# A new order of issue with a table of buffers, one pool of eight PSUM banks, and global scores issued tile by tile

## The chip, the cores and the metric

The kernel runs on one core of a Trainium2 chip, as one launch. The metric is the device time of an execution in microseconds (us). PE is TensorE, which runs the matmuls, PEld its weight loads, DVE VectorE, ACT ScalarE, POOL GpSimd, and SP the queue that issues nearly all DMAs. Each engine works through its own list of instructions in the order in which the kernel emits them, and waits on semaphores where it needs another engine's result or a buffer that another engine has yet to leave.

## What is computed

Three stages follow each other, with 4 batches of 544 tokens (512 local and 32 global) and 512 features:

```python
# 1. attention, 8 heads of 64: global queries see all keys, local ones a band of 65 and the 32 global keys
out_g = sm(scale * q_g @ k_all.T) @ v_all
s_ll = where(|i - j| <= 32, scale * q_l @ k_l.T, -1e9)
out_l = sm(concat(scale * q_l @ k_g.T, s_ll)) @ concat(v_g, v_l)
x = concat(out_g, out_l)
# 2. four experts, each a causal attention of width 64, weighted by a top-2 gate
for e in range(4):
    out += gate_e(x) * (softmax(causal(x @ wq[e], x @ wk[e])) @ (x @ wv[e])) @ wo[e]
# 3. a feed-forward with a token shift
xk = mu_k * x + (1 - mu_k) * x_prev
xr = mu_r * x + (1 - mu_r) * x_prev
return sigmoid(xr @ w_r) * (relu(xk @ w_k) ** 2 @ w_v)
```

(In the kernel local tokens stand ahead of global ones in a row of scores where that makes the band contiguous. Products that need more than one rounding's precision are made of three matmuls of a high and a low part.)

## The kernel before

All engine calls go to a recording layer. `Log` keeps each call as (engine, name, arguments) in a list, and tiles are `Lazy`: a tile is allocated when the first call that uses it is emitted. At the end `nc.emit(sequence(ORDER))` emits the calls in the order of the numbers in `ORDER`, a long table of steps between positions in the list. So `ORDER`, and nothing else, sets what stands behind what on each engine and in the DMA queue. The recording is done by ordinary loops:

- **Attention** (`a_` and `g_` functions). A pair P of heads has its queries and keys in one tile `kq{P}` (688 KB) and its values in `vw{P}`. `a_qk(n)` makes the local scores of a half pair: 8 matmuls into two tiles `S{n}_0` and `S{n}_1`, one for each head; DVE then masks and takes the minimum (`mn{n}`), ACT takes the exponential, DVE the reciprocal, POOL normalises (`pn{n}`, `glob`), PE transposes (`pT{n}`, and `pTg{u}` for `glob`), ACT or DVE copies the transposes out, and `a_pv(u)` multiplies by the values into `x{u}0`, `x{u}1` and `xg{u}`. `g_qk(u)` makes the global scores of two pairs (four heads): for each head a matmul of 32 x 512 into `Sga{u}` and one of 32 x 32 into `Sgb{u}`. Heads sit at partitions 0 or 64 of `kq`, and a head's 32 global queries fill 32 of the 128 rows of `Sga{u}`. So the four heads use four different places of PE's array: 64 rows by 32 columns each.
- **Experts** (`b_`, `c_`, `l_`, `e_`). `b_v` and `b_qk` make values (`pv`) and queries and keys (`pb..q`, `pb..k`). `c_qk(b, ep, i)` makes causal scores `C{b}{ep}{i}0` and `..1` of 128, 256, 384 or 512 columns; mask and minimum on DVE (`csm`, `cmn`), exponential on ACT, normalising on POOL, transposes `cT` on PE, copies `cpt` on ACT and DVE, and `c_pv` into `y`. `e_wo` (tiles `po`) is the output projection. Beside this stage the weights of stage 3 are loaded and split into a high and a low part (`wraw`, `wg`, `wy`) by ACT, DVE and POOL.
- **Feed-forward** (`d_`). Tokens in four blocks of 512 and one of 128: `d_mix` (tiles `m0`, `m1`), `d_k`, `d_v`, `d_r`, `d_out`.

PSUM has eight banks, and every tile in it fills one. `ps_s` and `ps_t` hand out six of them (tag `a`) in rotation: scores, transposes, projections. `ps_x` hands out two (tag `x`) to the accumulators of `a_pv`, `c_pv` and half of `d_v`. SBUF tags rotate in the same way: the n-th tile of a tag with k buffers takes the one that was handed out k tiles earlier. A matmul that starts a new tile waits until the last reader of the bank's former tile, a DVE or ACT instruction, is done.

Of the kernel before, what the change touches and what calls it, by code (L numbers as in the profile page):

```python
# [9 lines left out]
F32 = mybir.dt.float32  # L10
# [7 lines left out]
B, H, SL, SG, HD = 4, 8, 512, 32, 64  # L18
# [58 lines left out]
class LazyPool:  # L77

    def __init__(self, pool):
        self.pool = pool  # L80

    def tile(self, shape, dt, **kwargs):
        return Lazy(lambda: self.pool.tile(shape, dt, **kwargs), np.broadcast_to(np.float32(0), shape))
# [29 lines left out]
def chain_kernel(ctx: ExitStack, tc: tile.TileContext, kq, vw, vgd, wqkv, pack, wo, w_k, w_v, w_r, c_causal, out):  # L113
    nc = Log(tc.nc)
# [16 lines left out]
    def ps_s(name):  # L131
        return ps.tile([128, 512], F32, tag="a", bufs=6, name=name)

    def ps_t(name):
        return ps.tile([128, 512], F32, tag="a", bufs=6, name=name)

    def ps_x(name):
        return ps.tile([128, 512], F32, tag="x", bufs=2, name=name)
# [854 lines left out]
0 17 1 584 -592 -13 16 -17 13 -2 -2 -4 8 -21 8 2 -3 10 -19 1x2 1 -2 190 -195 18x2 1 44 -50 49 -46x2 96 -97x4 -8 7x3 1  # L993
21 99 -100x2 -26 25 -20 -3 2x2 153 -154 -8 -2 8x4 2 -14 14 67 -67 -16 8 11x4 -11 37x2 -7 -22 27x2 -8 7x2 -48 47x3 -10
-21x2 -8 -10 16x2 14 -15x4 22 2 -15 31 -44 -28 49 -23 -14 48 -9 -28 35x2 -51 40 9 -14 3 -26 -3 23 3 1 -32 29 1 30 -62
61x3 -34 4 53x4 -29 -26x4 -42 41x5 -28 34 9 -15 14 -19 18 -19 18 1 -15 -4 -2 4 13 1x2 -25 24x4 -21 20x3 -28 38 -11
10x3 141 -221 40 27 18x2 25 -49 22 -25 24 24 -38 54x2 -66 46 18x6 -78 15 2 34 -20 -19 18 -50 49x5 13 -14x2 -26 1 73
-48 109 -63 -73 72 -52 51 -49 49 -78 25 51x3 -12 11x4 -61 60x3 -89 88 -19 -32 -58 57x3 19 -54 61 17x2 -48 47 -86 85x8
-90 89 -41 40x2 -69 -24 44 19 -42 172 -173 377 -378 125 -103 102 -101 -53 152 -108 107 -102 -9 45x4 -69 68x2 -42 -23
63x6 -93 92 -69 68x3 -75 74x4 -95 94x3 -80 79x3 -70 69 79 -77 19 -88 -4 90 -19 -7x2 66 -42 28x2 11 -12x2 -53 29 -30 16  # L1000
-17x4 -11 10x3 24x2 30 -56 24x2 -28 4 22x2 -108 107x2 -29 2 5 -3 178 -177 24 -25 17 -18 -14 31 19 2 -19 -4 21x2 -44 43
-57 39x2 9 -10x2 84x4 -75 74 -88 87 -54 53x3 -93 92x3 -111 60x2 -61 60 -12 11 -48 -29 63 -36 46 -31x6 14 -15x2 2 -42
51 -3 -65 66x3 -14 2 20x2 14 -44 28x2 -24 23x2 11 -12x3 11 -47 35 30x2 44 -45x2 -27 26 -34 -4 36x3 -35 34x4 -63 20
41x2 -36 4x2 134 -135 -14 13 -7 -45 77x3 -30 29 -37 36x4 -40 39x3 -88 87x6 -76 75x2 31 -32x3 -80 79x3 -82 81 8x2 15
-145 128x2 68 -69x2 -80 79x2 2 -101 120 -36 -125 141 18x2 -24 49 -27x2 -29 -135 162x2 23 -24x2 -26 5 21 -22 -148 133
# [111 lines left out]
-25x11 -93 92 -93x11 16 -17 16x3 -19 18x3 -21 20x3 -23 22x2 4 -5 4x3 -7 6x3 -9 8x3 -11 10x26 50 -51 50x2 -26 25 -26x4  # L1117
22 -23x7 6 -7 6x2 -8 7 -8x2 12 -13 12 -8 7x2 -15 14
"""


def _constants():
    neg = np.float32(NEG)
# [67 lines left out]
```

## Time and profile before

| what | us |
|---|---|
| median of three runs | 554.11 |
| the three runs | 553.34 to 554.89 |
| the profiled execution | 553.6 |
| its span, first to last instruction | 551.8 |
| PE busy in the span | 524.6 (95%) |
| DVE, ACT, POOL busy | 319.5, 318.6, 303.7 (58%, 58%, 55%) |
| DMA: 51 MB, mean rate | 92 GB/s |

A busy share is the time in which at least one instruction of the engine is under way. A PE matmul is pipelined: the next may start before the last has ended, and the idle time that the profile names counts from the modelled end of the last. The chain of work that ended last lies on PE for 78% of the span. Attention ends at about 120 us, the experts at about 312 us, and the feed-forward takes the rest; the first two overlap for some 30 us, since `ORDER` mixes them.

### The profile page before, as it was taken

How to read it: one execution, taken by the hardware profiler on the slowest of the kernel's cores; microseconds unless marked ns; L12 is line 12 of the kernel's file. 1: busy time of each engine (PE TensorE's matmuls, PEld its weight loads, DVE VectorE, ACT ScalarE, POOL GpSimd, SP SyncE). 2: the span in 40 equal slices, each digit the busy share in tenths (PEclk: the TensorE clock that was granted, in tenths of full speed). 3: DMA queues.
4: the chain of work that ended last, by engine and by line, in shares of the span. 5: the costliest groups of instructions: out<-in, count | busy, mean ns of one | idle time of the engine just before them, and what ended most of it. 6: DMA issues, size and time to landing. Idle time of an engine off the chain costs nothing.

```text
span 551.8 us, 11621 instructions
## 1 busy us (share of the span) xinstructions
PE 524.6 (95%) x4286; PEld 429.8 (78%) x4286; DVE 319.5 (58%) x1065; ACT 318.6 (58%) x891; POOL 303.7 (55%) x361
## 2 busy tenths in 40 slices
PE   5899989999999999999798999999999999999996
PEld 2666677888878888888686788888888888888885
DVE  3667557587798879789878742415430367253011
ACT  4888567577677697687577664604541257233020
POOL 3768653738558888889677834505450376142110
PEclk9999999999999999799889999999999999999999
DMA  8958335005303454242722002001000100020002
GB/s 331 398 196 273 122 104 166 17 3 171 127 29 97 136 208 136 103 128 77 279 93 88 1 0 78 0 20 58 1 1 1 57 20 0 2 76 20 0 1 77
DMA packets 16025, 50.99 MB, mean 92 GB/s; under 512 B 1760, under 2 KB 2400, under 8 KB 15328
## 3 DMA queue, kind: packets, MB, share of 16 engines
q1 hardware_dynamic: 15680, 49.98, 25.9%
q8 instruction: 34, 0.56, 0.4%
q10 hardware_dynamic: 288, 0.26, 0.1%
q14 instruction: 23, 0.19, 0.1%
HBM read 39.49 MB, written 10.75 MB: 91 GB/s over the span
## 4 chain that ended last, share of the span: by engine, by line
PE 78%; DVE 9%; ACT 7%; POOL 3%; issue 1%; DMA 1%; ACTq 0%; DVEq 0%; POOLq 0%
PE v L100 17%; PE k L100 16%; PE r L100 8%; PE x L100 4%; PE S L100 4%; PE po L100 3%; PE pv L100 3%; PE y L100 3%; PE cT L100 3%; PE Sga L100 3%; PE C L100 3%; PE pT L100 2%; POOL csm L100 2%; ACT csm L100 2%; PE xg L100 1%; ACT sm L100 1%
## 5 line engine op out<-in xcount | busy, mean ns | idle before, releaser
L100 POOL TENSOR_TENSOR kk<-k,kk 128x512 fp32r<-128x512 f32 x32 | 41.7, 1311 | 92.9 <-ACT kk L100 92.8
L100 DVE TENSOR_TENSOR k<-k 128x512 f32<-128x512 f32 x34 | 29.3, 864 | 85.1 <-ACT k L100 84.6
L100 ACT ACTIVATE sm<-sm,mn 128x160 f32<-128x160 f32 x128 | 53.5, 420 | 24.4 <-DVE mn L100 21.0
L100 DVE SCALAR_TENSOR_TENSOR mm<-xT,small,mt 128x32 f32<-128x32 f32 (+7 forms) x64 | 48.5, 798 | 24.1 <-POOL m1cpt L100 12.5
L100 POOL TENSOR_TENSOR csm<-csm,crc 128x256 f32<-128x256 f32 (+3 forms) x64 | 51.9, 828 | 17.5 <-DVE crc L100 11.6
L100 POOL TENSOR_TENSOR pn<-sm,rc 128x256 f32<-128x256 f32 x64 | 38.6, 617 | 16.3 <-PE pT L100 6.5
L100 ACT ACTIVATE k<-k 128x512 f32<-128x512 f32 x34 | 20.3, 596 | 44.1 <-PE k L100 37.5
L100 DVE CUSTOM_DVE_ANT_0 sm<-S,band 128x160 f32<-128x160 f32 x128 | 35.2, 318 | 18.1 <-PE S L100 17.7
L100 PE MATMUL v<-wv1H,kk 128*128 128x512 f32 x136 | 43.6, 389 | 0.0
L100 PE MATMUL v<-wv0H,kk 128*128 128x512 f32 x136 | 43.5, 389 | 0.0
L100 ACT ACTIVATE csm<-csm,cmn 128x128 f32<-128x128 f32 (+3 forms) x64 | 35.8, 564 | 13.3 <-DVE cmn L100 12.9
L100 ACT ACTIVATE mt<-xT,omu 128x32 f32<-128x32 f32 (+7 forms) x64 | 31.6, 519 | 14.6 <-DVE mm L100 14.4
L100 POOL TENSOR_TENSOR m1cpt<-mm,m1vC 128x512 fp32r<-128x512 f32 x16 | 21.7, 1374 | 30.9 <-ACT m1vC L100 23.1
L100 DVE CUSTOM_DVE_ANT_0 csm<-C,causal 128x128 f32<-128x128 f32 (+3 forms) x64 | 29.9, 483 | 8.8 <-PE cT L100 4.8
L100 ACT CAST kk<-k 128x512 fp32r<-128x512 f32 x32 | 19.4, 620 | 24.2 <-PE v L100 13.6
L100 PE MATMUL S<-kq 64*64 64x160 f32 x512 | 27.1, 317 | 6.4 <-DMA kq<-in_kq_dram 4.9
L100 POOL TENSOR_TENSOR m0L<-mm,m0H 128x512 fp32r<-128x512 f32 (+1 forms) x20 | 25.2, 1271 | 14.2 <-ACT m0H L100 14.1
L100 DVE TENSOR_TENSOR rt<-v,rt 128x512 f32<-128x512 f32 x17 | 11.6, 686 | 36.0 <-PE v L100 26.3
L100 PE MATMUL y<-cpt,vC 128*64 128x128 f32 (+1 forms) x320 | 30.0, 313 | 2.2 <-DVE cpt L100 1.0
L100 PE MATMUL cT<-ident,csm 128*128 128x128 f32 x160 | 27.4, 288 | 4.2 <-POOL csm L100 2.0
L100 POOL TENSOR_TENSOR glob<-sm,rc 128x128 f32<-128x128 f32 x32 | 12.8, 403 | 33.9 <-DVE rc L100 23.1
L100 PEld LDWEIGHTS v<-wv0H,kk 128*128 128x128 f32 x136 | 25.5, 188 | 5.3
(316 smaller groups left out, 1582.8 us busy)
## 6 DMA issues: line engine op xcount, KB each, us to landing
kq<-in_kq_dram SPq DMA_DIRECT2D x15, 688.0 KB, 5.5
vw<-in_vw_dram SPq DMA_DIRECT2D x16, 512.0 KB, 4.5
out_dram<-rt SPq DMA_DIRECT2D x17, 256.0 KB, 2.0
wrawv<-in_moe_w_v_dram SPq DMA_DIRECT2D x8, 512.0 KB, 3.8
wrawk<-in_moe_w_k_dram SPq DMA_DIRECT2D x8, 512.0 KB, 4.1
wrawr<-in_moe_w_r_dram SPq DMA_DIRECT2D x4, 512.0 KB, 3.8
dv0H<-wgv SPq DMA_DIRECT2D x4, 256.0 KB, 2.8
dv0L<-wyv SPq DMA_DIRECT2D x4, 256.0 KB, 3.0
```

The lines of the kernel that those rows point to most:

```text
L100: getattr(getattr(self.nc, engine), name)(*[now(x) for x in args], **{k: now(x) for k, x in kwargs.items()})
```

## The change

Four things:

1. `LazyPool.tile` no longer lets a tag rotate. A table `SLOTS` names for each tag, tile by tile in the order of emission, which buffer it takes.
2. `ps_s`, `ps_t` and `ps_x` share one tag, `bank`, of eight banks; the table gives each of its 463 tiles one.
3. `g_qk` emits the four `Sga` matmuls of its four heads and then the four `Sgb`, where before each head's `Sgb` followed its `Sga`.
4. `ORDER` is a new table.

```diff
     def tile(self, shape, dt, **kwargs):
+        if kwargs.get("bufs", 1) > 1:
+            tag = kwargs["tag"]
+            n = self.count[tag] = self.count.get(tag, -1) + 1
+            kwargs.update(tag=tag + SLOTS[tag][n], bufs=1)
         return Lazy(lambda: self.pool.tile(shape, dt, **kwargs), np.broadcast_to(np.float32(0), shape))
...
     def ps_s(name):
-        return ps.tile([128, 512], F32, tag="a", bufs=6, name=name)
+        return ps.tile([128, 512], F32, tag="bank", bufs=8, name=name)
...
     def ps_x(name):
-        return ps.tile([128, 512], F32, tag="x", bufs=2, name=name)
+        return ps.tile([128, 512], F32, tag="bank", bufs=8, name=name)
...
-        for pp in range(2):
-            t = kqs[2 * u + pp]
-            for h in range(2):
-                rr = slice(64 * h, 64 * h + 64)
-                oo = slice(32 * (2 * pp + h), 32 * (2 * pp + h) + 32)
-                k = t[rr, KT0:KT0 + 768].rearrange("p (g c) -> p g c", c=96)[:, :, 0:64]
-                nc.tensor.matmul(sa[oo, :], t[rr, QG0:QG0 + SG], k, start=True, stop=True)
-                nc.tensor.matmul(sb_[oo, 0:SG], t[rr, QG0:QG0 + SG], t[rr, KT0 + 64:KT0 + 96], start=True, stop=True)
+        hs = [(kqs[2 * u + n // 2], slice(64 * (n % 2), 64 * (n % 2) + 64), slice(32 * n, 32 * n + 32)) for n in range(4)]
+        for t, rr, oo in hs:
+            k = t[rr, KT0:KT0 + 768].rearrange("p (g c) -> p g c", c=96)[:, :, 0:64]
+            nc.tensor.matmul(sa[oo, :], t[rr, QG0:QG0 + SG], k, start=True, stop=True)
+        for t, rr, oo in hs:
+            nc.tensor.matmul(sb_[oo, 0:SG], t[rr, QG0:QG0 + SG], t[rr, KT0 + 64:KT0 + 96], start=True, stop=True)
...
 ORDER = """
-0 17 1 584 -592 -13 16 -17 13 -2 -2 -4 8 -21 8 2 -3 10 -19 1x2 1 -2 190 -195 18x2 1 44 -50 49 -46x2 96 -97x4 -8 7x3 1
...
+SLOTS = {
...
+    "kp": "03210321032103210321",
...
```

What the new order does is read from the built programs. In the rows below a number behind a tile's letter is its index in the kernel (`Sga3` is `g_qk(3)`), and the number behind the last underscore is the tile's own. The line is that of the recording layer, and it stands four lines lower in the changed kernel. `x2` is two equal instructions in a row.

PE in the first third of attention, around the global scores of pairs 6 and 7, before:

```order
L100 MATMUL pT9_820<-ident_105,pn9_710 128x128 x4
L100 MATMUL Sga3_834<-kq6_345 32x512
L100 MATMUL Sgb3_836<-kq6_345 32x32
L100 MATMUL Sga3_834<-kq6_345 32x512
L100 MATMUL Sgb3_836<-kq6_345 32x32
L100 MATMUL Sga3_834<-kq7_405 32x512
L100 MATMUL Sgb3_836<-kq7_405 32x32
L100 MATMUL Sga3_834<-kq7_405 32x512
L100 MATMUL Sgb3_836<-kq7_405 32x32
L100 MATMUL x10_620<-tg1_655,vgb_152 128x512
```

and now:

```order
L104 MATMUL xg1_589<-ptlg_103,vw2_182 64x32
L104 MATMUL Sga3_712<-kq6_311 32x512 x2
L104 MATMUL Sga3_712<-kq7_364 32x512 x2
L104 MATMUL Sgb3_720<-kq6_311 32x32 x2
L104 MATMUL Sgb3_720<-kq7_364 32x32 x2
L104 MATMUL S12_0_726<-kq6_311 64x160
```

The four 32x512 matmuls now stand in one row. Before, `g_qk(3)` and `g_qk(6)` alone had their two pairs side by side; the two pairs of each of the other six stood apart, 8 to 130 matmuls of other work between them, and once a pair of one call stood beside a pair of another. Now all eight calls have the form shown.

PE later in attention, at local scores that take over a bank, before (`S19_0` takes the bank of `S18_1`, and `pv00` that of `S19_0`):

```order
L100 MATMUL pT15_1201<-ident_105,pn15_1098 128x128 x4
L100 MATMUL S18_0_1210<-kq9_706 64x160
L100 MATMUL S18_1_1212<-kq9_706 64x160
...
L100 MATMUL S19_0_1225<-kq9_706 64x160
L100 MATMUL S19_1_1227<-kq9_706 64x160
...
L100 MATMUL pv00_1241<-wv_929,x00_1094 128x260 x12
```

and now (`pv00` takes the bank of `Sga5`, and `S19_0`, further down, that of `pb01k0`):

```order
L104 MATMUL S18_1_1147<-kq9_664 64x160
L104 MATMUL Sga5_1162<-kq10_963 32x512 x2
L104 MATMUL Sga5_1162<-kq11_944 32x512 x2
L104 MATMUL Sgb5_1174<-kq10_963 32x32 x2
L104 MATMUL Sgb5_1174<-kq11_944 32x32 x2
L104 MATMUL pb01q0_1179<-x00_1113,wq_412 128x256 x12
L104 MATMUL pv00_1205<-wv_1036,x00_1113 128x260 x12
L104 MATMUL pb01k0_1231<-x00_1113,wk_818 128x256 x12
L104 MATMUL pv01_1257<-wv_1036,x00_1113 128x260 x12
L104 MATMUL pT14_1281<-ident_111,pn14_1109 128x128 x4
```

The projections have moved in between. Before, no matmul stood between the last one into `S18_1` and the first into `S19_0`, and one between `S19_0` and `pv00`; now 16 stand between `Sga5` and `pv00`, and 24 between `pb01k0` and `S19_0`.

PE in the experts' stage, where the scores of batch 3 begin, before (`C3011` takes the bank of `cT2120`):

```order
L100 MATMUL cT2120_4427<-ident_105,csm2120_4273 128x128 x3
L100 MATMUL cT2111_4434<-ident_105,csm2111_4214 128x128 x2
L100 MATMUL pb31k1_4438<-x31_4183,wk_763 128x288 x12
L100 MATMUL cT2121_4471<-ident_105,csm2121_4237 128x128 x3
L100 MATMUL C3010_4485<-qk30_3873 128x256
L100 MATMUL C3011_4487<-qk30_3873 128x256
```

and now (`C3011` takes the bank of `y203`):

```order
L104 MATMUL y203_4444<-cpt203_4175,vC2_3312 64x160 x8
L104 MATMUL y203_4444<-ptl2_4298,vl_2551 64x32 x2
L104 MATMUL C3000_4467<-qk30_3905 128x128
L104 MATMUL C3001_4469<-qk30_3905 128x128
...
L104 MATMUL cT2121_4483<-ident_111,csm2121_4245 128x128 x3
L104 MATMUL cT2120_4490<-ident_111,csm2120_4260 128x128 x3
L104 MATMUL C3010_4503<-qk30_3905 128x256
L104 MATMUL C3011_4505<-qk30_3905 128x256
```

The bank that `C3011` takes over was emptied before by ACT, and now by ACT and DVE, with 13 matmuls between where there were 18.

Counted over both whole programs: a bank passes from one tile to the next 455 times. Fewer than 6 matmuls stood in between 11 times before and never now, fewer than 12 matmuls 53 times before and 16 times now. Between the local scores of a half pair and their transposes stood 99 matmuls (median of 32), now 141; the fewest were 24 and are 48. Between causal scores and their transposes stood 92 (median of 64), now 111; the fewest were 46 and are 56. On DVE, as its list is printed with equal rows in one, 135 rows lay between the first mask of `C200` and that of `C300`, and 126 do now.

## Rows read from the trace of the kernel before

**Rows 1.** Table by stretch: us, busy (instructions) per engine, granted PE clock, DMA share, GB/s

```profile
0.00:120.00 120.00, 108.46 (x1580) 79.06 (x1581) 74.52 (x424) 82.79 (x314) 69.67 (x131) 1.00 0.52 185
120.00:200.00 80.00, 77.69 (x795) 68.02 (x795) 64.70 (x240) 58.46 (x166) 57.99 (x66) 1.00 0.36 117
200.00:312.00 112.00, 103.06 (x819) 87.62 (x818) 96.22 (x290) 84.80 (x227) 89.03 (x94) 0.94 0.35 123
312.00:547.00 235.00, 234.87 (x1097) 195.01 (x1096) 82.72 (x115) 92.54 (x186) 87.01 (x71) 1.00 0.06 21
```

**Rows 2.** PE's waits, whole run: waiting group <- releaser, us in total, times, longest

```profile
PE S L100 <- DMA kq<-in_kq_dram: 4.9, 1, 4.9
PE pT L100 <- POOL pn L100: 2.4, 2, 1.5
PE C L100 <- ACT cpt L100: 1.9, 1, 1.9
PE C L100 <- DVE qk L100: 1.4, 1, 1.4
...
PE pv L100 <- DVE mn L100: 0.9, 1, 0.9
```

**Rows 3.** Groups by line and form, global scores: busy us, mean ns, idle before

```profile
L100 PE MATMUL Sga<-kq 64*32 64x512 f32 x64 | 17.4, 630 | 0.0
L100 PE MATMUL Sgb<-kq 64*32 64x32 f32 x64 | 4.3, 195 | 0.3 <-DVE mng L100 0.3
```

**Rows 4.** PE timeline, three calls of global scores: start, us, group, idle before

```profile
9.42 1.06 PE L100 MATMUL Sga<-kq 64*32 64x512 f32 x4
...
10.47 1.32 PE L100 MATMUL S<-kq 64*64 64x160 f32 x32
...
44.11 1.04 PE L100 MATMUL Sga<-kq 64*32 64x512 f32 x2
...
46.11 0.70 PE L100 MATMUL x<-tg,vgb 64*128 64x512 f32 x2
...
90.94 1.38 PE L100 MATMUL Sga<-kq 64*32 64x512 f32 x8
...
92.31 0.34 PE L100 MATMUL x<-pt,vw 128*64 128x64 f32 x4
```

**Rows 5.** PE timeline in attention, at local scores that wait for their banks

```profile
67.52 1.18 PE L100 MATMUL S<-kq 64*64 64x160 f32 x16
69.60 1.28 PE L100 MATMUL S<-kq 64*64 64x160 f32 x16 [0.89 <-DVE mn L100]
71.75 1.31 PE L100 MATMUL pv<-wv,x 128*128 128x260 f32 x9 [0.87 <-DVE mn L100]
```

**Rows 6.** PE timeline in the experts' stage, at the scores of batch 3

```profile
269.46 0.38 PE L100 MATMUL C<-qk 64*128 64x256 f32 x1
271.74 0.62 PE L100 MATMUL C<-qk 64*128 64x256 f32 x5 [1.90 <-ACT cpt L100]
```

**Rows 7.** ACT timeline ahead of and during the same wait

```profile
268.26 0.73 ACT L100 ACTIVATE csm<-csm,cmn 128x512 f32<-128x512 f32 x1 [4.02 <-DVE cmn L100]
...
270.57 0.62 ACT L100 CAST wk1H<-wyk 128x512 fp32r<-128x512 f32 x1
271.21 0.48 ACT L100 COPY cpt<-cT 128x384 f32<-128x384 f32 x1
```

**Rows 8.** Table by stretch, as Rows 1: two at half the clock, and what encloses them

```profile
221.10:227.90 6.80, 6.37 (x40) 4.23 (x38) 5.85 (x22) 4.58 (x15) 5.33 (x8) 0.50 0.20 75
272.30:279.10 6.80, 5.97 (x38) 4.60 (x38) 5.00 (x19) 3.98 (x13) 3.92 (x6) 0.50 0.67 264
218.70:274.00 55.30, 49.81 (x401) 42.61 (x399) 48.11 (x142) 39.42 (x107) 45.30 (x48) 0.92 0.40 138
```

**Rows 9.** DMA issues: the causal mask's load, KB, us from issue to landing

```profile
causal<-in_causal_dram SPq DMA_DIRECT2D x1, 256.0 KB, 4.6
```

More of the change, by code (lines that the diff above doesn't have):

```diff
@@ L79, in __init__ @@
     def __init__(self, pool):
-        self.pool = pool
+        self.pool, self.count = pool, {}
     def tile(self, shape, dt, **kwargs):
+        if kwargs.get("bufs", 1) > 1:
+            tag = kwargs["tag"]
+            n = self.count[tag] = self.count.get(tag, -1) + 1
+            kwargs.update(tag=tag + SLOTS[tag][n], bufs=1)
         return Lazy(lambda: self.pool.tile(shape, dt, **kwargs), np.broadcast_to(np.float32(0), shape))
@@ L131, in ps_s @@
     def ps_s(name):
-        return ps.tile([128, 512], F32, tag="a", bufs=6, name=name)
+        return ps.tile([128, 512], F32, tag="bank", bufs=8, name=name)
     def ps_t(name):
-        return ps.tile([128, 512], F32, tag="a", bufs=6, name=name)
+        return ps.tile([128, 512], F32, tag="bank", bufs=8, name=name)
     def ps_x(name):
-        return ps.tile([128, 512], F32, tag="x", bufs=2, name=name)
+        return ps.tile([128, 512], F32, tag="bank", bufs=8, name=name)
     ident = const.tile([128, 128], F32, name="ident")
@@ L992 @@
 ORDER = """
-0 17 1 584 -592 -13 16 -17 13 -2 -2 -4 8 -21 8 2 -3 10 -19 1x2 1 -2 190 -195 18x2 1 44 -50 49 -46x2 96 -97x4 -8 7x3 1
[L994 to L1002, printed above, removed]
@@ new lines @@
+-60 -39 38x3 -49 48x4 54 -55x2 -57 2 53x3 52 -53 43 -44x3 -63 62 37 -38x4 -71 70x2 -57 -16 178 -104 -61x3 -47x2 194
+-150 -46 137 -138 218x2 -220 131 87x2 -87 86x4 -62x2 -40 39x2 25 -26x4 60 -105 67 -101 75 176 -174 1 -82 76 -77 193x2
+-68 67x4 -70 -56 124x4 -72 71x2 -127 19x3 -70 69 -63x3 88 -89 92 -85x2 -10 32 -24 42 -43x3 23 -24 78 -42 -38x2 -60
+59x2 118 -119 75 -34 75 -76 -44 43x2 25 -26 27 -28 -47 46x2 -11 10x2 69 -70x2 15 -84 89x2 200 -201x2 -15 14 -94 113x2
+-49 64 -17 -23 22x5 94x4 72 -171 97 -20 19x3 2 -72x2 73 -74x2 -26 93 -69x2 71 -72x5 65 -66x4 63 -64x2 -44 43x2 113
@@ new lines @@
+244 -185 184x3 -248 247x2 -289 39 -40x3 37 -38x6 60 -61x3 58 -59x4 55 -56x3 53 -54x4 50 -51 50 50 -51x2 22 -23 48 -103
+53x2 20 -21x5 84x5 114 -115x7 -40x12 -52 51 -52x3 49 -50x8 16 25 -26x3 -6 5 22 -23x5 -11 10 69 -70 16 52 -53x3 20
+-21x3 18 -19x5 16 25 -26x3 -6 5x3 -8 7x5 15x25 67x3 -13 12 -13x2 -8 7 -8 17 -18 7 -8 7 -3 2x2 -10 9
+"""
+SLOTS = {
+    "vC": "0101010101010",
+    "rep": "010110",
+    "kp": "03210321032103210321",
+    "raw": "01010101010101010101010101010101010",
+    "csm0": (
+        "0321032103210321032103210321032103210321032103210321032103210321032103210321032103210323232103"
+    ),
+    "y": "01010101100110010101010101010101",
+    "wy": "01010101010101010101010101010101010101010101010101010101010101",
+    "csm1": "01010101010101010101010101010101010101010101010101010",
+    "cpt": "010101010101010101010101010101010101010101010101",
+    "wo": "01010101",
+    "wg": "010101010101010101010101010101",
+    "qk": "021022210210210",
+    "mn": "02102102102102102102102102102102",
+    "su": "03120312031203120312031203120312",
+    "mng": "01010101",
+    "sug": "01010101",
+    "rc": "02102102102102102102102102102102",
+    "rcg": "01010101",
+    "lg": "0101",
+    "gate2": "0101",
+    "cmn": "02102102102102102102102102102102",
+    "csu": "02102102102102102102102102102102",
+    "crc": "02102102102102102102102102102102",
+    "bank": (
+        "012367034551273546037256401635470127352120713537640533575770012571256302541665715240603627142507"
+        "451370330507364166273354015445405212167032614630417570573215201530746156472627065761451034232466"
+        "757040334502377731440316722073406556344735645760437503421466370651274015430354110026375620727656"
+        "653170675401024022131252563277340070264720415563723421643757106700560314534376121745261252547271"
+        "6017726435517070110032635074104717705415272107674373326313164030751024225573257361601724"
+    ),
+}
```

240 lines of the change are left out of this document (124 added, 116 removed).

## The prediction, made before the changed kernel was timed

> **What bounds the kernel now.** I read the table by stretch first, with the boundaries of the stages as its cuts [rows 1]. The reader should look at PE's column. In the feed-forward (312 to 547 us) PE is busy 234.87 of 235.00 us at the full clock: nothing that an order of issue moves can be gained there, and PE's instructions there are the same in number. Attention up to 120 us has 11.5 us in which PE idles, the stretch from 120 to 200 us 2.3, and the experts' stretch from 200 to 312 us 8.9. So PE bounds the whole kernel, and what there is to gain lies in three places: its idle time of 22.8 us, the time in which its clock is low (0.94 in the third stretch), and PE work that could overlap better.
>
> Next come PE's waits [rows 2]. The longest, 4.9 us, is the first load of `kq`, at the very start; the new order still begins with that load, so it stays. That leaves 6.6 us of idle time in attention. The other rows name what PE waited for: `pT` for POOL's `pn` is a wait for data, whereas `C` behind ACT's `cpt`, and `pv` behind DVE's `mn`, read nothing of the tile named. They wait for the bank that this engine has yet to leave. So two kinds of wait exist here, and the new table and the new order touch both.
>
> The idle time shown is a lower bound of what a wait costs, since it counts from a modelled end. A row of 16 local-score matmuls takes about 0.66 us when two follow one another (32 in 1.32 us) [rows 4]; from one such row to the next with a bank wait it took 69.60 - 67.52 = 2.08 us [rows 5], a loss of 1.42 where 0.89 is shown. I use the shown figures for the forecast, and their ratio, 1.6, for the far end.
>
> The third look is at the clock. Two stretches, from 221.1 to 227.9 and from 272.3 to 279.1 us, were granted 0.50, which is the level of 1.2 GHz, with 1.00, that of 2.4 GHz, around them [rows 8]. The second begins 0.6 us after PE resumed from the longest wait of the stage, 1.90 us for ACT's `cpt` [rows 6]; the first follows the wait of 1.4 us behind DVE's `qk` [rows 2] in the same way. Such a stretch costs half of the PE work done in it: 6.37 / 2 = 3.2 us and 5.97 / 2 = 3.0 us [rows 8], 6.2 us together.
>
> **The change part by part.**
>
> *Global scores.* Eight calls, four heads each. Before, `Sga` fills 17.4 us of PE; `Sgb` with 4.3 us lies nearly all beside it [rows 3]. A pair of heads takes 10.47 - 9.42 = 1.05 us until the next work starts, its `Sgb` included [rows 4], and most pairs stand alone, so a call pays about 2.1 us. Now four `Sga`, at four places of the array, stand in one row. What four heads cost is seen twice, in the old order of emission: from 90.94 to 92.31 us, 1.37 us, where all eight instructions of the four `Sga` ran as one group, and from 44.11 to 46.11 us, 2.00 us, where they did not run as one [rows 4]. The near end is that four heads take what two do, 1.06 us. So eight calls cost between 8 x 1.06 = 8.5 and 8 x 2.00 = 16.0 us. I take 1.1 us a call, near the low end, since the new order lacks what stood between the long matmuls at 44.11 us, the short `Sgb`: 8.8 us, a gain of 17.4 - 8.8 = **8.6 us** (bounds 1.4 and 8.9). It only counts where PE is the bound; up to 120 us DVE has 45 us free, ACT 37 and POOL 50 [rows 1], so I count it in full.
>
> The Trainium skill, in "TensorEngine Tiling (Array Packing)", under its restrictions, says that different row tiles can't access one PSUM bank at the same time. Heads 0 and 1 of a pair are two row tiles, and all four write one bank. By that rule the quads would bring nothing. The trace disagrees as far as it goes: the group at 90.94 us is four heads of one bank in 1.38 us, where two take 1.06 [rows 4].
>
> *Eight banks in one pool and the table.* No instruction is added, and a buffer named in a table costs nothing by itself. What changes is who waits for whom. Where `pv00` waited 0.87 us and a row of `S` 0.89 us for DVE's `mn` [rows 5], none or one matmul stood between the bank's two tiles, and now 16 and 24 do; the twelve of a projection alone take over 1.31 us (nine of them do [rows 5]), so those waits should go. The data waits in attention, 2.4 us for `pn` at the start [rows 2], have more local scores ahead of them now (a minimum of 48 matmuls between scores and transposes, where 24 stood). Of the 6.6 us in attention I take **5.0**, and leave 1.6 for the start, where little work is loaded yet. Bounds: 0, since a wait may only move to the next place, and 6.6 x 1.6 = 10.6. From 120 to 200 us I take **1.5** of 2.3 (0 to 3.7).
>
> *The experts.* `C3011` waited 1.90 us since ACT's copy of `cT2120`, which frees its bank, stood behind an exponential that had itself waited 4.02 us for DVE's minimum, and behind a cast of 0.62 us for a weight of stage 3 [rows 6, 7]. The new bank of `C3011` comes from `y203`, which ACT and DVE leave earlier, and 13 matmuls stand in between: this wait goes, unless `y203`'s own readers stand behind the same queue. The wait behind `qk` should go in the same way, since causal scores now have 56 matmuls or more until they are needed. With both waits I let both half-speed stretches go: **6.2 us** (bounds 0 and 6.8, half of the two spans of 6.8). Of the 8.9 us of idle time there [rows 1] I take only **3.0**. The reason is DVE: it is busy 96.22 of the 112 us, and 48.11 of 55.30 in the part around the waits [rows 1, 8], and the change removes none of its work. The stage can't get shorter than DVE's 96.2 us, so 15.8 us is the end of what there is, and near it PE waits for masks and minima again. With 6.2 + 3.0 the stage would take 102.8 us, with DVE busy for 94% of it; more than that I do not believe in.
>
> *Loads.* The same DMAs are issued; `SP`'s list moves `kq1` to `kq3` ahead of values, and the causal mask's load, 256 KB, takes 4.6 us to land [rows 9]. It takes over the buffer of the band mask, so it waits for the last DVE mask of attention, and the first causal scores are needed soon after. DVE may idle some 2.4 us there. I cost it at nothing, since the local and global work still to be done in the overlap covers PE; without that cover it costs up to 4.6 us less what DVE does meanwhile, so I keep 2.4 for the range.
>
> The sum is 8.6 + 5.0 + 1.5 + 6.2 + 3.0 = 24.3 us. Profiled, the kernel before took 553.6 us (a span of 551.8), 0.5 less than the median of 554.1: 553.6 - 24.3 = 529.3, and 529.8 as a median, **530 us**.
>
> **The rivals.**
>
> *Everything goes.* Score 8.9, attention's waits at their far end 10.6, the middle 3.7, and the experts' stage down to DVE's own time, 15.8: 39.0 us, 515 us. For it speaks that no bank passes on with fewer than 6 matmuls in between any more; against it that DVE would have to work without a gap.
>
> *DVE holds the experts' stage.* The two waits vanish, but PE waits later for the same DVE work, so from 200 to 312 us nothing is gained: 554.1 - 15.1 = 539 us. DVE's 86% [rows 1] speaks for it; against it that the clock's share alone is not DVE's.
>
> *Waits only move.* The scores bring 8.6 us and the rest evens out: 545.5 us. It speaks for this that 22.8 us of idle time in 552 are few and made of many short waits, of which [rows 2] show the longest, and that 13 to 16 matmuls of cover are a few us.
>
> *The quads run as pairs.* By the group at 44.11 us the scores gain 1.4 us only, the rest as forecast: 554.1 - 1.4 - 15.7 = 537 us. The rule quoted above is this case; the group at 90.94 us speaks against it.
>
> *Slower.* The order puts bank or data waits behind a long queue of ACT or DVE in the experts' stage, each like the one at 271.74 us: 1.90 us of idle time and a stretch at half clock, 1.9 + 3.1 = 5.0 us. While the two old ones go, new ones must come to as many and more: with no gain in waits elsewhere, and the scores' 8.6 us kept, two further ones beyond the old number give 545.5 + 10.0 = 555.5, three 560.5 us. So it decides from the second on. For it speaks that cover got shorter at places (13 for 18 at `C3011`, 126 rows of DVE for 135 between first masks) and that DVE is the fullest feeding engine; against it that the long distances grew in the median.
>
> That the change doesn't do what it says is excluded: the built program has the quads, and the banks of the table.
>
> **How the numbers follow.** The forecast has a chance of 0.48, everything goes 0.09, DVE holds 0.14, waits only move 0.13, quads as pairs 0.04, slower 0.12. About 0.3%, 1.7 us, is what a measurement of this kernel can tell from no change. Of the slower case 0.09 lies beyond that and 0.03 within it; of the moved waits 0.01 comes within it, with the others faster: faster 0.87, same 0.04, slower 0.09. The range leaves out the slower case and about half of the one in which everything goes: 515 to 547 us, with the 2.4 us of the mask inside it. The forecast's own range is 523 to 538 us.
>
> **What would show it right or wrong.** In the profile after, `Sga` should be busy some 9 us instead of 17.4, in eight groups of about 1.1 us. If a group shows about 2 us, the quads run as pairs. PE's waits should hold no row `S` or `pv` behind `mn`, and no `C` behind `cpt` or `qk` of over 1 us; the granted clock between 200 us and the end of the experts should be 1.00 throughout. If a stretch at 0.50 remains, look at the wait just ahead of it: about 3 us each are then missing. DVE's busy share in the experts' stage should rise to about 94%, its sum stay the same; if PE waits for `csm` and `cmn` in small pieces instead, the rival on DVE is right. The feed-forward should take 235 us as before. The forecast fails as a whole if PE's idle time ahead of the feed-forward is not reduced by some 9 us.

## The result: 515.8 us, and the profile after

| | median us | runs |
|---|---|---|
| before | 554.5 | 553.3 to 556.0 |
| changed | 515.8 | 514.8 to 518.0 |
| ratio | 0.931 | 95% interval 0.927 to 0.935 |

In a second group of runs, on another chip, the changed kernel's median was 519.6 us (515.9 to 520.8), so differences of less than 4 us between its variants below say nothing. The profiled execution took 515.4 us, with a span of 513.6. Three statements of the part on the change are wrong: the table counts a tag's tiles in the order in which they are recorded, not emitted; the pools of before did not hand out their buffers strictly in turn, as the built program shows; and the kernel has 472 tiles in PSUM, each with an entry in the table, not 463 (so a bank passes on 464 times).

The table by stretch is cut once more, now at points of equal PE work, so that the two kernels can be laid side by side: after about 850 of PE's matmuls, after about 1,875, at the first matmul of the feed-forward (`k`), and at the last `po`. Columns as in [rows 1]. The kernel before:

```profile
0.00:65.90 65.90, 56.81 (x852) 37.73 (x853) 38.79 (x237) 48.65 (x184) 42.18 (x83) 1.00 0.72 262
65.90:140.70 74.80, 71.76 (x1025) 59.69 (x1022) 51.08 (x246) 48.70 (x173) 43.70 (x68) 1.00 0.31 101
140.70:303.60 162.90, 152.24 (x1288) 130.46 (x1285) 138.79 (x454) 121.93 (x336) 124.00 (x136) 0.96 0.37 125
303.60:337.10 33.50, 33.37 (x207) 28.05 (x206) 16.95 (x29) 17.71 (x41) 16.91 (x15) 1.00 0.00 1
```

The changed kernel:

```profile
0.00:52.30 52.30, 46.82 (x848) 34.91 (x848) 38.97 (x231) 45.26 (x172) 39.12 (x77) 1.00 0.86 328
52.30:119.30 67.00, 65.84 (x1026) 56.32 (x1023) 49.70 (x254) 51.95 (x189) 44.72 (x73) 1.00 0.36 115
119.30:265.30 146.00, 142.40 (x1280) 128.17 (x1278) 134.74 (x446) 118.06 (x325) 126.96 (x135) 1.00 0.39 133
265.30:299.10 33.80, 33.66 (x209) 28.80 (x210) 17.08 (x37) 19.58 (x48) 17.62 (x17) 1.00 0.09 32
```

The same work takes 13.6, 7.8 and 16.9 us less in the first three rows, 0.3 more in the fourth: 38.0 us, all of it ahead of the point where only the feed-forward is left. In each of the first three rows PE's idle time (length less busy) falls, and so does its busy time, for nearly the same number of matmuls. The clock column of the third row goes from 0.96 to 1.00.

PE's waits, as in [rows 2], and the groups that answer to [rows 3], of the changed kernel:

```profile
PE S L104 <- DMA kq<-in_kq_dram: 4.0, 1, 4.0
PE cT L104 <- POOL csm L104: 2.5, 3, 1.6
PE xg L104 <- ACT ptlg L104: 1.2, 1, 1.2
PE pTG L104 <- DVE rc L104: 0.8, 1, 0.8
PE pTg L104 <- POOL glob L104: 0.3, 1, 0.3
PE C L104 <- ACT cpt L104: 0.3, 1, 0.3
```

```profile
L104 PE MATMUL Sga<-kq 64*32 64x512 f32 x64 | 8.9, 624 | 0.0
L104 PE MATMUL Sgb<-kq 64*32 64x32 f32 x64 | 1.9, 191 | 0.0
```

No `S` and no `pv` waits for `mn` any more, `C` has one wait of 0.3 us left of the 1.9 and 1.4, and `Sga` is busy for half as long. A call of the global scores on PE's timeline, to be held against [rows 4] (start, us, group):

```profile
27.21 1.06 PE L104 MATMUL Sga<-kq 64*32 64x512 f32 x8
28.09 0.24 PE L104 MATMUL Sgb<-kq 64*32 64x32 f32 x8
28.27 1.03 PE L104 MATMUL S<-kq 64*64 64x160 f32 x21
```

From its start to the next work a call takes 28.27 - 27.21 = 1.06 us, with all four heads in it. Six of the eight calls take 1.05, the first two 1.42 and 1.12: 8.8 us, where the thirteen pieces of before took 17.8 in the same measure.

### The profile page after: what moved, and what is told of

The parts are those of the page before. It is cut to its first block, busy times and chain, and to the rows that moved or that the text cites. A ratio compares the mean times of both kernels' runs of the same rounds, so it can differ in the third digit from the quotient of the medians.

```text
span 513.6 us, 11622 instructions
## 1 busy us (share of the span) xinstructions
PE 499.5 (97%) x4286; PEld 422.1 (82%) x4286; DVE 312.6 (61%) x1065; ACT 316.7 (62%) x891; POOL 304.8 (59%) x361
## 4 chain that ended last, share of the span: by engine, by line
PE 77%; DVE 7%; POOL 6%; ACT 4%; DMA 3%; issue 1%; SPq 0%; POOLq 0%; DVEq 0%; ACTq 0%
PE k L104 18%; PE v L104 18%; PE r L104 9%; PE x L104 5%; PE S L104 3%; PE po L104 3%; PE y L104 3%; PE pv L104 3%; PE pT L104 2%; POOL csm L104 2%; PE cT L104 2%; PE xg L104 2%; PE C L104 2%; PE Sga L104 1%; DVE csm L104 1%
## 5 line engine op out<-in xcount | busy, mean ns | idle before, releaser
L104 POOL TENSOR_TENSOR kk<-k,kk 128x512 fp32r<-128x512 f32 x32 | 43.2, 1357 | 97.2 <-ACT kk L104 94.6
L104 DVE TENSOR_TENSOR k<-k 128x512 f32<-128x512 f32 x34 | 27.3, 807 | 74.4 <-ACT k L104 74.1
L104 POOL TENSOR_TENSOR csm<-csm,crc 128x128 f32<-128x128 f32 (+3 forms) x64 | 52.1, 833 | 16.3 <-DVE crc L104 13.8
L104 ACT ACTIVATE sm<-sm,mn 128x160 f32<-128x160 f32 x128 | 53.7, 421 | 10.2 <-DVE mn L104 8.4
L104 PE MATMUL v<-wv1H,kk 128*128 128x512 f32 x136 | 44.9, 390 | 0.0
L104 ACT ACTIVATE mt<-xT,omu 128x480 f32<-128x480 f32 (+7 forms) x64 | 31.5, 517 | 16.7 <-DVE mm L104 16.6
L104 PEld LDWEIGHTS v<-wv1H,kk 128*128 128x128 f32 x136 | 25.5, 188 | 5.3
L104 PEld LDWEIGHTS x<-pt,vw 128*64 128x64 f32 x512 | 24.7, 137 | 5.1 <-issue 1.7
L104 PE MATMUL cT<-ident,csm 128*128 128x128 f32 x160 | 25.3, 280 | 2.9 <-POOL csm L104 2.5
L104 PE MATMUL S<-kq 64*64 64x160 f32 x512 | 23.5, 320 | 4.1 <-DMA kq<-in_kq_dram 4.0
L104 POOL TENSOR_TENSOR x<-xT,x 128x256 fp32r<-128x256 f32 (+1 forms) x32 | 24.3, 780 | 5.1 <-ACT x L104 3.6
```

Source lines behind the costliest of these rows:

```text
L104: getattr(getattr(self.nc, engine), name)(*[now(x) for x in args], **{k: now(x) for k, x in kwargs.items()})
```

## The experiments

The runs came in four groups, each on one chip and beside the kernel before, which took 554.7 us in each. Theory A is the forecast: scores, bank waits and half-speed stretches are separate terms, and DVE holds the experts' stage soon after. Its rivals were that the feeding engines bind, that waits only move, and that quads run as pairs.

### Global scores alone, in the kernel before

```diff
         sb_ = ps_s(f"Sgb{u}")
-        for pp in range(2):
...
+        for t, rr, oo in hs:
+            k = t[rr, KT0:KT0 + 768].rearrange("p (g c) -> p g c", c=96)[:, :, 0:64]
+            nc.tensor.matmul(sa[oo, :], t[rr, QG0:QG0 + SG], k, start=True, stop=True)
...
 ORDER = """
-0 17 1 584 -592 -13 16 -17 13 -2 -2 -4 8 -21 8 2 -3 10 -19 1x2 1 -2 190 -195 18x2 1 44 -50 49 -46x2 96 -97x4 -8 7x3 1
+0 17 1 584 -585x2 176 -176x2 -12 -13 24 44 -50 49 52 -101 -12 144 -142 180 -198 8 -12 15 -5 2 -7x2 -8 23x3 -25 24x5
...
```

> The kernel before with one edit: each call of the global scores emits its four Sga and then its four Sgb in one row, at the place where its second pair stood; banks, buffers and all other instructions stand as before. If four heads run beside each other and PE bounds attention (the forecast's first term), Sga falls from 17.4 to about 9 us busy and the time by about 8.6 us, to 546 us. If the engines that feed attention set its pace, Sga falls as much but PE's waits grow in its place: 551 to 555 us. If the quads run as pairs, Sga stays at 16 us or more and the time within 2 us of before.

547.0 us, ratio 0.987 (0.985 to 0.989): 7.7 us less. `Sga` fell to:

```profile
L104 PE MATMUL Sga<-kq 64*32 64x512 f32 x64 | 10.5, 658 | 0.0
```

The first call, which the order put at 7.1 us into the start, cost 3.1 us there, the others 1.05 to 1.13. The waits of `pT`, `C`, `S` and `pv` stayed: 2.4 us for `pn`, up to 1.4 for `qk` and for `cpt`, 0.9 each for `mn`. So the term stands by itself, PE bounds attention, and pairs it is not.

This run also shows what the emission inside a call is worth. In `g_qk(3)` and `g_qk(6)` the two pairs stood side by side already, so there the edit only puts the four `Sgb` behind the four `Sga` instead of one behind each. These are the two calls that took 2.00 and 1.37 us before [rows 4]. Here:

```profile
41.97 1.06 PE L104 MATMUL Sga<-kq 64*32 64x512 f32 x8
42.91 0.26 PE L104 MATMUL Sgb<-kq 64*32 64x32 f32 x8
43.10 1.13 PE L104 MATMUL x<-tg,vgb 64*128 64x512 f32 x4
...
85.87 1.06 PE L104 MATMUL Sga<-kq 64*32 64x512 f32 x8
86.75 0.24 PE L104 MATMUL Sgb<-kq 64*32 64x32 f32 x8
86.92 0.34 PE L104 MATMUL x<-pt,vw 128*64 128x64 f32 x4
```

They take 1.13 and 1.05 us until the next work: 0.9 and 0.3 us less, with nothing else changed in these calls.

### The old emission of a call, in the changed kernel

```diff
-        for t, rr, oo in hs:
-            k = t[rr, KT0:KT0 + 768].rearrange("p (g c) -> p g c", c=96)[:, :, 0:64]
-            nc.tensor.matmul(sa[oo, :], t[rr, QG0:QG0 + SG], k, start=True, stop=True)
...
+                nc.tensor.matmul(sa[oo, :], t[rr, QG0:QG0 + SG], k, start=True, stop=True)
+                nc.tensor.matmul(sb_[oo, 0:SG], t[rr, QG0:QG0 + SG], t[rr, KT0 + 64:KT0 + 96], start=True, stop=True)
...
```

> The changed kernel with one edit: a call of the global scores emits for each head Sga and then Sgb, as before the change, at the same place; table, banks and all else as in the changed kernel. If four Sga must stand in one row to run beside each other, Sga goes back to about 16 us and the time rises by 6 to 8 us, to 522 to 524 us. If it is enough that the two pairs stand together (as at 90.94 us of the kernel before, 1.37 us a call), the calls take 1.1 to 1.4 us and the time rises by 0 to 3 us, to 516 to 519 us.

519.0 us (518.6 to 520.2), but the edit did not reach the program. It changes the order in which a call is recorded, and `ORDER` was written anew with it. In the built program PE's list is that of the changed kernel, matmul for matmul, with four `Sga` ahead of four `Sgb` in all eight calls; the lists of the other engines are the same too, and every tile takes its bank or buffer over from the same tile as there. So this is the changed kernel once more, and neither of the two expectations was tested. PE's timeline has the call of the changed kernel:

```profile
29.91 1.06 PE L104 MATMUL Sga<-kq 64*32 64x512 f32 x8
30.79 0.24 PE L104 MATMUL Sgb<-kq 64*32 64x32 f32 x8
30.96 0.77 PE L104 MATMUL S<-kq 64*64 64x160 f32 x16
```

What the third of the four edits is worth with the new order stays unmeasured; the two calls of the run before speak for the forecast's view that `Sgb` between the `Sga` costs time.

As a repeat the run tells two things. First, the call stands 2.7 us later than in the changed kernel (29.91 for 27.21 us): PE waits twice for `kq` at the start here, 5.3 us in all instead of 4.0, and the first call of scores takes 1.97 us instead of 1.42. So more than half of the 4.8 us between the two profiled executions (520.2 and 515.4) is lost at the start. Second, one wait is followed by two different clocks. PE's `cT` waits for POOL's `csm` at the same place of the same list, in the changed kernel and here:

```profile
152.76 0.55 PE L104 MATMUL cT<-ident,csm 128*128 128x128 f32 x3 [1.64 <-POOL csm L104]
```

```profile
155.09 0.55 PE L104 MATMUL cT<-ident,csm 128*128 128x128 f32 x3 [1.50 <-POOL csm L104]
...
157.00:160.30 3.30, 3.30 (x16) 3.05 (x16) 1.65 (x11) 2.67 (x10) 3.30 (x4) 0.50 0.50 192
```

In the changed kernel's execution the clock stayed at 1.00 behind the longer wait; here it fell to 0.50 for about 3.4 us behind the shorter one.

### Eight banks and a table, with the old order

```diff
-        return ps.tile([128, 512], F32, tag="a", bufs=6, name=name)
+        return ps.tile([128, 512], F32, tag="bank", bufs=8, name=name)
...
-        return ps.tile([128, 512], F32, tag="x", bufs=2, name=name)
+        return ps.tile([128, 512], F32, tag="bank", bufs=8, name=name)
...
```

(`ORDER` is written anew here as well, with every engine's list as in the kernel before.)

> The kernel before with its order of every engine's list unchanged, and its eight banks in one pool: each tile takes, by a table, the bank that has been free longest (a rough count, not the table of the changed kernel). SBUF buffers as before. If bank waits and what follows them are worth what the forecast says, the waits of S, pv and C behind mn, cpt and qk go, and with them one or both stretches at half clock: 8 to 12 us less, 543 to 547 us. If the banks matter only together with the new order (an engine's list still brings the reader too late), the waits move to data: within 3 us of before, 551 to 555 us.

548.9 us, ratio 0.992 (0.988 to 0.995): 5.8 us less by the medians, 3 to 6 by the interval, and so between the two expectations. The waits:

```profile
PE pT L104 <- POOL pn L104: 2.8, 3, 1.5
PE y L104 <- DVE cpt L104: 2.4, 2, 1.8
...
PE S L104 <- DVE mn L104: 0.9, 1, 0.9
PE pv L104 <- DVE mn L104: 0.9, 1, 0.9
```

The 1.9 us of `C` behind ACT's `cpt` are gone, but a data wait of `y` for 1.8 us appeared, and `S` and `pv` still wait 0.9 each: `S19_0` and `pv00` still take over a bank with none and one matmul in between, since with that order the rule finds none that is free earlier by its count. Stretches at half clock moved and became shorter; there are five, among them these:

```profile
69.50:73.00 3.50, 2.84 (x13) 2.87 (x14) 1.57 (x13) 1.86 (x8) 0.00 (x0) 0.56 0.57 201
270.50:274.50 4.00, 4.00 (x34) 3.42 (x30) 2.81 (x12) 2.60 (x12) 2.62 (x3) 0.60 0.60 247
```

### A rough table in place of the changed kernel's

```diff
     "bank": (
-        "012367034551273546037256401635470127352120713537640533575770012571256302541665715240603627142507"
+        "012367034551273546037256401653470127532120715357640355373770021372136521360443703162425417061320"
...
```

(378 of its 472 entries differ: each tile takes the bank that has been free longest. But much of this is only another numbering of the banks: 386 of the 464 times, a tile takes the bank over from the same tile as by the changed kernel's own table. `ORDER` has other numbers here and in the next run, with every engine's list unchanged.)

> The changed kernel with its order and its SBUF table, and the banks by the rule of e_bank8 (the bank free for longest by a rough count) in place of its own table. If the table is a part of the gain in its own right, banks chosen by the rough rule bring late readers back and the time rises by 3 us or more, to over 520 us. If any sensible table of eight banks does, it stays at 515 to 520 us, where two chips put the changed kernel.

519.4 us (517.5 to 520.1): no difference that can be read. So the 78 hand-overs in which the two tables differ carry no gain that shows. What the new order would do with the six and two banks of before was not run.

### Late banks on purpose

```diff
     "bank": (
...
-        "0734065563447356457604375034214663706512740154303541100263756207"
+        "0734265563447356457604375234014663721560742654323546622013751027"
...
```

(A stretch of the table; 161 entries differ, since the two banks change places from there on.)

> The changed kernel with only the table of banks altered: at four places of the experts' stage a tile takes over a bank whose reader ends late, by the changed kernel's trace 2.5 us (C1030 after Ll1), 2.2 us (po031 after po021), 2.2 us (pb31q0 after cT2001) and 1.9 us (C3000 after pb30q1) after the tile's first matmul began there; every engine's list is the same. By the forecast's price each place costs its wait and a stretch at half clock, some 2.2 + 3 us: about 21 us in all, 536 us. If a wait costs only itself, 8 to 9 us: 524 us, the clock at 1.00 throughout. If PE has slack there because DVE sets the pace of the stage, PE catches up: 516 to 519 us.

526.0 us: 523.6 and 523.9 us in two runs with a mean clock of 0.997, 528.2 and 529.1 in two with 0.993 and 0.990. All four waits stand in the list of waits as meant:

```profile
PE C L104 <- DVE lmn L104: 2.5, 1, 2.5
PE pb31q L104 <- DVE cpt L104: 2.0, 1, 2.0
PE po L104 <- ACT xT L104: 2.0, 1, 2.0
PE C L104 <- DVE ql L104: 1.9, 1, 1.9
```

Behind two of them the clock fell, behind the other two it did not. The stretches behind the waits, which end at 162.6, 184.2, 221.3 and 251.6 us (the first two columns are the stretch and its length, the granted clock is the third from the end):

```profile
162.80:166.20 3.40, 3.40 (x17) 2.69 (x18) 0.66 (x1) 0.00 (x0) 2.26 (x3) 0.50 0.23 89
184.00:191.00 7.00, 6.79 (x70) 5.73 (x70) 4.49 (x14) 5.82 (x17) 6.42 (x8) 1.00 0.36 108
221.00:228.00 7.00, 6.72 (x56) 6.75 (x57) 4.22 (x9) 3.46 (x11) 5.10 (x4) 1.00 0.20 75
251.60:258.30 6.70, 6.69 (x40) 5.18 (x40) 3.60 (x15) 2.13 (x8) 3.15 (x3) 0.50 0.20 83
```

The run on the old emission has the changed kernel's lists and hand-overs and comes from the same chip. Against it the four waits cost 7.0 us by the medians (526.0 and 519.0), and 8.9 us between the two profiled executions (529.1 and 520.2), with 8.4 us of shown waits and two half-speed stretches where the other has one. That is near the second expectation, the waits alone, though not with the clock at 1.00. The price of 5 us a place is too high: it takes the wait and the stretch as one, and a wait of 2 us need not bring a stretch. That PE catches up for nothing falls as well.

### The order, half by half

Three hybrids and a mirror: the order of one kernel up to a point, then all that is left in the relative order of the other, banks and buffers by the rough rule. The pools are those of the changed kernel; beyond that, and the emission of the global scores where the new order takes them up, only tables of numbers change (here, one that begins with the old order):

```diff
 ORDER = """
-0 17 1 584 -592 -13 16 -17 13 -2 -2 -4 8 -21 8 2 -3 10 -19 1x2 1 -2 190 -195 18x2 1 44 -50 49 -46x2 96 -97x4 -8 7x3 1
+0 17 1 584 -585x2 176 -176x2 -12 -13 24 44 -50 49 52 -101 -12 144 -142 180 -198 8 -12 15 -5 2 -7x2 -8 23x3 -25 24x5
...
```

> A hybrid: the changed kernel's order up to the last instruction of attention (118 us there), then what is left in the relative order of the kernel before; banks and buffers by a table of the same rule as in e_bank8. If the order of the experts' remainder carries the gain in that stage (waits and clock, 9 to 13 us), the time is 525 to 529 us, with stretches at half clock after 200 us. If the gain was made up to there, by attention alone and by experts' work started earlier within it, 516 to 519 us.

> The other hybrid: the order of the kernel before up to the last instruction of attention (142 us there; pairs of global scores apart), then what is left in the relative order of the changed kernel; banks and buffers by the same rule as in e_bank8. If the order of the experts' remainder carries 9 to 13 us, the time is 541 to 545 us (e_bank8, without it, 549). If the gain is made in attention, it is as e_bank8, 547 to 551 us.

> A third hybrid: the order of the kernel before up to its first matmul of S18 (PE is at about 66 us there, 855 of its matmuls done), then all that is left in the relative order of the changed kernel, the later half of attention included; banks and buffers by the rule of e_bank8. Its two neighbours measured 539.4 us (e_headB_tailA, cut at the end of attention) and about 517 to 519 us (all in the new order). If the gain of attention lies in the bank waits around 66 to 73 us and in the global scores behind them, some 9 to 12 of these 21 us, the time is 528 to 531 us. If it lies in the first half (the start, data waits for pn, and twelve of the pairs of global scores), less than 6 us are gained here: 534 to 539 us.

> The mirror of e_cut18: the order of the changed kernel up to its first matmul of S18 (about 52 us), then all that is left in the relative order of the kernel before; banks and buffers by the rule of e_bank8. From e_cut18 (534.1 us) the first part of attention is worth some 15 to 18 us to the changed kernel. If that gain is made there and stays made, the time is e_bank8's 549 less 15 to 18 us: 531 to 534 us. If it is made there only because the later order takes it up (work in flight at the cut), the time is 537 us or more.

They took 532.5, 539.4, 534.1 and 543.3 us (the last 541.0 to 548.0). The first lies above both of its expectations, the second below both of its own; the third lies at the edge of its second one. From the old order to the new in steps from the end backwards:

| kernel | new order from | us | step |
|---|---|---|---|
| before | nowhere | 554.7 | |
| eight banks | nowhere | 548.9 | 5.8 |
| hybrid | end of attention | 539.4 | 9.5 |
| hybrid | `S18` | 534.1 | 5.3 |
| changed | the start | 515.8, 519.6 | 14 to 18 |

The last step also takes in the changed kernel's own table of SBUF buffers, which was not tried alone. It can't be worth much in attention: with the new order up to there and the rough rule for buffers, the first hybrid's experts' row begins at 121.3 us (below), the changed kernel's at 119.3. From the other side, new order up to `S18` gives 543.3 and up to the end of attention 532.5, so what a part is worth depends on what stands behind it. The mirror missed its first expectation of 531 to 534 us. In its trace PE has done 832 matmuls by 52.3 us, where the changed kernel has done 848 and the kernel before needed 65.9 us for 852; so the lead is there, and it is lost in part just behind the cut, where only 94 follow in 13.7 us:

```profile
52.30:66.00 13.70, 9.68 (x94) 6.70 (x95) 5.80 (x34) 5.93 (x26) 5.60 (x12) 0.88 0.35 125
```

There PE is idle for 4.0 us, 2.1 of them in a wait of `pT` for a `pn`, and the granted clock is 0.88: the cut made a wait of its own. The hybrid with the old remainder keeps the lead of attention, but the experts then take 161.1 us for 1,284 matmuls, as before (162.9):

```profile
121.30:282.40 161.10, 152.10 (x1284) 132.25 (x1282) 137.89 (x453) 120.70 (x331) 126.03 (x135) 0.97 0.38 125
```

With the new remainder behind the old attention they take 153.4, with both new 146.0. So both halves of the new order carry gain, and the experts do best when attention is new as well.

### DVE's work in the experts' stage

```diff
+            for _ in range(2 if n in self.twice else 1):
+                getattr(getattr(self.nc, engine), name)(*[now(x) for x in args], **{k: now(x) for k, x in kwargs.items()})
...
+            if e == 0:
+                nc.twice.add(len(nc.ops))
             nc.vector.tensor_tensor_reduce(out=t[:, :w], in0=st[e][:, :w], in1=causal[:, 512 - w:], op0=ALU.add,
```

> The changed kernel with extra work: of each pair of causal masks (csm out of C) DVE does the first one twice, 32 instructions and 30.1 / 2 = 15 us of DVE time more, all in the experts' stage. If DVE sets the pace of that stage, as the forecast held it would once PE's waits were gone (94% busy), the time rises by 8 to 15 us, to 524 to 531 us. If PE still sets it and DVE has some slack at each place, by 0 to 4 us.

> The kernel before with the same extra work as e_dve: of each pair of causal masks DVE does the first one twice, 15 us of DVE time more in the experts' stage, where DVE is 86% busy. e_dve cost the changed kernel about 6 us. If DVE's slack is what the new order used up, the extra work costs less here, 0 to 4 us: 555 to 558 us. If DVE's work lies on the path as much before as after, 5 to 8 us: 560 to 563 us.

The changed kernel went to 525.7 us, 6.0 over its 519.6 on the same chip (8.7 between the two profiled executions there), and the kernel before to 562.4, 7.7 over its 554.7. By its rise the first lies between its two expectations; the second lies in its upper one. The doubled masks add 15.6 and 15.8 us to their own rows, but DVE's busy time rose by 10.1 and 10.2 us only (312.6 to 322.7 and 319.5 to 329.7). So most of what DVE was given shows in the time, in both kernels, and the medians can't tell the two apart.

The stretch that the forecast looked at, the 820 or so matmuls ahead of 312 us in the kernel before, tells more. With the extra work, first the changed kernel, then the kernel before:

```profile
182.40:285.00 102.60, 96.97 (x821) 84.20 (x821) 96.26 (x325) 82.01 (x223) 87.22 (x92) 1.00 0.34 117
```

```profile
205.30:321.30 116.00, 103.05 (x819) 87.61 (x818) 102.33 (x331) 85.55 (x227) 87.12 (x94) 0.96 0.35 119
```

Without it the stretch takes 95.8 us with 90.05 us of DVE's work in the changed kernel (row further down) and 112.0 us with 96.22 before [rows 1]. So 6.2 us more of DVE's work make it 6.8 us longer in the changed kernel, where DVE stays 94% busy, and 6.1 us more make it 4.0 us longer before. It is one execution of each. It fits the forecast's view that DVE holds the stage once PE's waits are gone. Whether PE would go faster with less DVE work was not tried.

The repeat of the changed kernel, which gave the 519.6 us:

> The changed kernel once more, on the same chip as the three beside it, so that differences of 2 or 3 us between its variants can be read. Same chip or not makes no difference: 514.5 to 518 us. If a chip moves the start (the first kq lands later or the first global scores run at half clock), up to 519 us.

It missed both of its expectations. Its four executions alone span 515.9 to 520.8 us, so the chip need not be the cause.

## Why the prediction was right in sign and too small

Forecast were 530 us, in a range of 515 to 547; measured were 515.8, only 0.8 us inside its lower end. The gain is 38.7 us where 24.3 was the sum. In the two profiled executions it can be laid out by the forecast's own terms (38.0 us up to the last `po`):

| term | forecast | measured |
|---|---|---|
| global scores | 8.6 | 8.9 (17.8 to 8.8) |
| half-speed stretches | 6.2 | both gone (clock 1.00 after), 6.2 by the forecast's own estimate |
| idle time that the profile shows | 9.5 | 12.5 (22.9 to 10.4; 0.9 of it at the start) |
| less busy time for the same matmuls, beyond these two | 0 | 10.4 |

- **Scores: right in size, and in reason as far as it was tested.** Four heads do run in the time of two, and the gain counts in full since PE bounds attention (the run of the scores alone: 7.7 us). The forecast put it down to the four `Sga` standing in one row without `Sgb` between them. The two calls in which only the emission changed, 2.00 to 1.13 us and 1.37 to 1.05, bear it out; why `Sgb` between them cost 0.9 us in one and 0.3 in the other is not settled. The rival of pairs falls: eight instructions of four heads and one bank in 1.06 us. The Trainium skill's "TensorEngine Tiling (Array Packing)", under its restrictions, doesn't hold here in the words quoted ahead: heads 0 and 1 are two row tiles that write one bank in the same microsecond.
- **Bank waits: right where they were named.** `S`, `pv` and `C` no longer wait behind `mn`, `cpt` and `qk`. But the forecast put "eight banks in one pool and the table" ahead of the order; alone the eight banks bring some 3 to 6 us, since with the old order `S19_0` and `pv00` still wait, and another table made no difference. The rest came with the new order, which was only run with eight banks.
- **Half-speed stretches: right, with some luck.** They went with the two waits that had preceded them. But the changed kernel has a wait of 1.6 us of its own in this stage, and such a wait was followed by half clock in the run on the old emission. Three of the changed kernel's four executions had a mean clock of 1.00, the fourth 0.993 and 518.0 us.
- **The term that was mis-sized is the waits.** The step was: "I use the shown figures for the forecast, and their ratio, 1.6, for the far end". The shown idle time fell by 12.5 us, three more than forecast, and the time of the same matmuls beyond that, scores and clock taken out, by another 10.4, for which the forecast had nothing. The ratio of the two together to the shown part is 1.8, above even the far end. By the forecast's own stretches, cut where PE has done as many matmuls as in [rows 1], the changed kernel has:

```profile
0.00:100.30 100.30, 94.82 (x1580) 75.50 (x1581) 76.02 (x442) 83.77 (x322) 71.19 (x134) 1.00 0.60 221
100.30:179.40 79.10, 75.60 (x794) 68.08 (x792) 66.42 (x226) 59.50 (x165) 60.60 (x66) 1.00 0.43 141
179.40:275.20 95.80, 94.54 (x822) 83.75 (x821) 90.05 (x285) 80.61 (x222) 87.20 (x91) 1.00 0.37 125
```

- **Where the miss lies.** Attention gained 19.7 us (13.6 forecast), the middle 0.9 (1.5), the experts' stretch 16.2 (9.2). With the scores' 8.9 us taken out, attention's waits gave 10.8 where 5.0 was taken and 10.6 was the far end. The middle's idle time even grew, from 2.3 to 3.5 us, while the experts' fell from 8.9 to 1.3.
- **That all of the 10.4 us are waits is argued, not shown.** For it speaks that the busy time of `S` fell from 27.1 to 23.5 us for the same instructions (rows below), and that rows as [rows 5] lose more than they show. Against it: where four waits were put in on purpose, 8.4 us shown cost 7 to 9. PE also changes less often from one kind of matmul to another (from `S` to others 17 times for 24). What part each has stays open.
- **DVE: the share was right, the work was not.** The forecast took only 3.0 of the 8.9 us of idle time in the experts' stretch, since "the change removes none of its work" and the stage "can't get shorter than DVE's 96.2 us"; at 102.8 us DVE would be 94% busy. DVE is 94% busy now, but at 95.8 us: its work for these matmuls is 90.0 us where it was 96.2, in 285 instructions for 290. The bound held for a fixed amount of work, and that amount changed with the order; how, no run separates.
- **Rivals.** "Everything goes", 515 us with a chance of 0.09, came nearest, and stretch by stretch: 8.9 for the scores, 10.6 for attention's waits and 15.8 for the experts, where 8.9, 10.8 and 16.2 came. Its condition, DVE at work without a gap, was not needed, since DVE's work shrank. "Slower" didn't come, since no long wait was put behind a queue; the four late banks show that it would have taken more places than two, as the four cost 7 to 9 us together, stretches included. The mask's load cost nothing: DVE waits for no DMA in the changed kernel.

The rows on the busy time, first of before, then of the changed kernel (line, engine, group, busy us, mean ns, idle ahead and its releasers):

```profile
L100 PE MATMUL S<-kq 64*64 64x160 f32 x512 | 27.1, 317 | 6.4 <-DMA kq<-in_kq_dram 4.9 <-DVE mn L100 1.1 <-ACT ptlg L100 0.2
L100 PE MATMUL y<-cpt,vC 128*64 128x128 f32 x192 | 18.8, 317 | 1.0 <-DVE cpt L100 1.0
```

```profile
L104 PE MATMUL S<-kq 64*64 64x160 f32 x512 | 23.5, 320 | 4.1 <-DMA kq<-in_kq_dram 4.0
L104 PE MATMUL y<-cpt,vC 128*64 128x128 f32 x192 | 15.4, 282 | 0.4 <-DVE cpt L104 0.2
```

For `S` the mean of one instruction is the same (317 and 320 ns) while the group's busy time is 3.6 us less: the instructions lie closer, and the loss had been inside "busy". For `y` the mean falls too: 40 of the matmuls from `cpt` into `y` stood in the two half-speed stretches of before, so its fall belongs to their term and not to the 10.4 us.

## What to carry to other kernels

Where PE is "95% busy", lay two stretches of equal matmul count side by side, or one against its best repeat: the shown idle time that went, 12.5 us, was about half of what the new order took out beside the scores. Matmuls that use different parts of the array are worth bringing together in the order, with no short ones between them: two calls that already stood together lost 0.9 and 0.3 us by the latter alone. A pool with more banks pays little until the order leaves a bank free at the place that waits. An engine's work in a fixed stretch of the old time is no bound for the new one: count it again for the same matmuls. And where a table sets the order of issue, an edit to the recording alone can leave the program as it was.

## What the hardware showed that was not expected

Four heads at four places of the array, two row tiles and four column tiles, all writing one bank, took 1.05 us, as two heads do. With short matmuls emitted between them two such calls took 2.00 and 1.37 us, and 1.13 and 1.05 with the short ones behind. After PE waits of 1.9 to 2.5 us the granted clock fell to 1.2 GHz in two cases of four; before the change it had done so behind waits of 1.4 and 1.9 us. Behind one and the same wait it fell in one execution (1.50 us) and stayed at 2.4 GHz in another (1.64 us). The changed kernel's medians in two groups of runs differ by 3.8 us (515.8 and 519.6), those of the kernel before by 0.2 (554.5 and 554.7).
